# Running the first MLP's first product plainly on the first three token tiles

## The chip, the core and the metric

The kernel runs on one core of one Trainium2 chip. The metric is the device time of one execution in microseconds (us). The median of three runs of the kernel before is 1400.02 us (1398.33 to 1400.51).

The core has five engines with a queue each, which work in order and wait for each other by semaphores: TensorE (PE in the rows, its weight loads PEld), VectorE (DVE), ScalarE (ACT), GpSimd (POOL) and SyncE (SP), which issues all transfers of this kernel.

## The reference

Attention with a softmax over the features of q and over the positions of k, and then two MLPs on its output, all in float32 (the weights of the MLPs arrive as 64-bit floats):

```python
q_s = softmax(q, axis=-1)            # q, k, v: 8 batches, 8 heads, 576 positions, 64
k_s = softmax(k, axis=2)
x   = q_s @ (k_s^T @ v)              # -> 4608 tokens x 512
h   = x @ w_in                       # 512 x 2048
g   = max(h, 0) + alpha * min(h, 0)
x   = g @ w_out                      # 2048 x 512
h   = x @ w2_in                      # 512 x 1024
out = layernorm(h * softmax(h)) * g_ln @ w2_out
```

## The kernel before

**Tiles and stages.** The 4608 tokens are nine tiles of 512 (`NTL`). The first MLP runs in two phases (`ph`), each over half of the 2048 hidden features, and in a phase each tile `i` is worked in two units `u` of 512 features. For a tile and a unit there are a first product (`g1`, into the PSUM banks `ga` and `gx`), the leaky function (`leaky`), a split of its result into two parts (`split_g`, tiles `gg0` and `gg1`), and a second product (`g2`), which adds into four banks `acc`. `finish` copies `acc` to `p_d` in HBM when a tile's two units are done in phase 0; phase 1 adds to that.

**Products in three passes.** All MLP operands are held as a high part in a shorter float format (`F32R`) and the remainder (`put`: ScalarE writes the high part, VectorE or GpSimd subtracts). Each product is high by high, high by low and low by high: three matmuls.

**The first product by seven block products.** `g1` multiplies 512 x 512 blocks with seven products of half-size blocks rather than eight, with block sums of the weights (`S1` to `S4`, made by `w_in_ops`) and of the tokens (`T1` to `T4`, made by `x_prep`). It is issued in four parts, 84 matmuls of 256 columns in all for a tile and unit. `keep` copies three partial results out of PSUM, and VectorE adds them (L248, L256, L258).

**Weights.** `load_w64` brings a 512 KB piece of a 64-bit weight into a raw tile with one transfer on SP's queue, ScalarE turns its high words into floats (L109), and three VectorE instructions (L110 to L112) repair sign and low bits. Then `put` splits it. For phase 0 there are 16 such pieces, four of w_in and four of w_out for each unit. Unit 0's eight are loaded ahead of the tile loop (`boot_w`), and their splits and block sums are put on GpSimd (`G`). Unit 1's eight are loaded in `hook0` in the first three slots of tile 0 (`second_in`, `second_out`), all through one raw buffer: the tag `rn` of the pool `gp`, which has one buffer. `leaky` takes its tile `rn` from the same tag.

**Attention in the slots.** Each tile has eight slots, and the steps of attention for batches 1 to 7 are dealt out to the slots of phase 0. Batch 0 runs ahead of the loop, and tile 0's slots hold all of batch 1 and the start of batch 2. `q_x` makes x and sends it to `x_d` in HBM; for tile 0 it also keeps it in SBUF (`xraw`). The tile `xf`, from which it is sent, has two buffers, and `k_max` of a later batch uses the same two.

**The order.** The program is written in the order of the functions `phase` and `slot`, and a scheduling layer then interleaves the independent pieces on each engine. The order in which the instructions stand on an engine is fixed when the program is built.

## Time and profile before

| | |
|---|---|
| median of three runs | 1400.02 us |
| the profiled execution | 1404.14 us, span 1402.4 us |
| TensorE busy, over the span | 1314.6 us, 94% |
| VectorE busy | 1025.6 us, 73% |
| ScalarE busy | 781.5 us, 56% |
| GpSimd busy | 62.0 us, 4% |
| mean granted clock of TensorE | 0.966 |

A share of the span is an average over stages: batch 0's attention and the weights (to about 50 us), tile 0 (to 197 us), the tiles of phase 0 with attention beside them (to about 512 us), the rest of phase 0, phase 1, and the second MLP. "Busy" of an engine is the union of its instructions' times, and instructions of one engine overlap a little, so the distance between starts is shorter than the length.

### The profile page before, as it was taken

What the parts mean: (1) busy time and instruction counts of PE and PEld (TensorE: products, weight loads), DVE (VectorE), ACT (ScalarE), POOL (GpSimd) and SP (SyncE); (2) the same over time, 40 slices, a digit from 0 to 9 for tenths busy, and PEclk for the clock granted to TensorE, in tenths of its full rate; (3) what the DMA queues carried; (4) which work ended last, traced back from release to release, by engine and by line L of the source; (5) the groups of instructions that cost most, each with busy time, mean ns of one, the idle gap of its engine ahead of it and who ended that gap; (6) DMA issues with size and microseconds to landing.
All of it is one profiled execution on the core that took longest, in us unless ns stands there. A gap on an engine that the chain in (4) does not pass through costs nothing.

```text
span 1402.4 us, 19636 instructions
## 1 busy us (share of the span) xinstructions
PE 1314.6 (94%) x7428; PEld 1131.9 (81%) x7428; DVE 1025.6 (73%) x1730; ACT 781.5 (56%) x1323; POOL 62.0 (4%) x74
## 2 busy tenths in 40 slices
PE   3656899999999999999999999999999999999998
PEld 3544788889898888888888888898788888888886
DVE  6988688889888677797778755545877676766653
ACT  5534655665665656585556645444556455555543
POOL 0612100000000000000000000000000000000000
PEclk8675799999999999999999999999999999999999
DMA  8464224544352433424545422138121111112011
GB/s 181 126 169 144 81 78 127 144 142 119 119 145 65 138 106 128 138 81 141 183 157 195 166 63 88 46 122 274 67 64 38 53 51 41 58 34 61 31 31 30
DMA packets 127919, 148.10 MB, mean 106 GB/s; under 512 B 55504, under 2 KB 94416, under 8 KB 125648
## 3 DMA queue, kind: packets, MB, share of 16 engines
q1 hardware_dynamic: 127824, 146.85, 34.8%
q8 instruction: 58, 0.95, 0.3%
q14 instruction: 37, 0.30, 0.1%
HBM read 99.63 MB, written 47.19 MB: 105 GB/s over the span
## 4 chain that ended last, share of the span: by engine, by line
PE 72%; DVE 10%; DMA 7%; ACT 5%; issue 2%; POOL 1%; SPq 0%; ACTq 0%; DVEq 0%
PE acc L291 7%; PE acc L292 7%; PE acc L290 7%; PE o L897 5%; PE o L899 5%; PE o L898 5%; PE ga L225 4%; PE ga L227 3%; PE ga L226 3%; PE gx L225 2%; PE gx L226 2%; PE gx L227 2%; PE h2a L833 2%; PE h2a L835 2%; PE h2a L834 2%; PE tp L889 2%
## 5 line engine op out<-in xcount | busy, mean ns | idle before, releaser
L291 PE MATMUL acc<-gg,w 128*128 128x512 f32 x576 | 230.2, 400 | 1.9 <-DVE gg L117 1.9
L290 PE MATMUL acc<-gg,w 128*128 128x512 f32 x576 | 229.2, 401 | 2.7 <-ACT gg L116 2.6
L292 PE MATMUL acc<-gg,w 128*128 128x512 f32 x576 | 229.5, 398 | 0.0
L271 DVE SCALAR_TENSOR_TENSOR t<-rn,nalpha,t 128x512 f32<-128x512 f32 x144 | 102.1, 747 | 48.1 <-ACT t L268 47.8
L291 PEld LDWEIGHTS acc<-gg,w 128*128 128x128 f32 x576 | 109.4, 190 | 24.4 <-DVE gg L117 2.7
L292 PEld LDWEIGHTS acc<-gg,w 128*128 128x128 f32 x576 | 109.3, 190 | 24.4
L290 PEld LDWEIGHTS acc<-gg,w 128*128 128x128 f32 x576 | 108.7, 189 | 24.0 <-ACT gg L116 3.2
L267 ACT ACTIVATE rn<-t 128x1024 f32<-128x1024 f32 x72 | 75.7, 1051 | 73.2 <-DVE t L258 72.7
L897 PE MATMUL o<-wo,lt 128*128 128x512 f32 x288 | 114.4, 397 | 0.3 <-ACT lt L116 0.3
L899 PE MATMUL o<-wo,lt 128*128 128x512 f32 x288 | 114.2, 397 | 0.0
L898 PE MATMUL o<-wo,lt 128*128 128x512 f32 x288 | 114.1, 396 | 0.0
L116 ACT ACTIVATE gg<-t 128x1024 fp32r<-128x1024 f32 x72 | 76.4, 1061 | 36.7 <-DVE t L271 35.9
L117 DVE TENSOR_TENSOR gg<-t,gg 128x1024 fp32r<-128x1024 f32 x72 | 87.9, 1220 | 11.3 <-ACT gg L116 11.0
L225 PE MATMUL ga<-xT,w_S 128*128 128x256 f32 x288 | 84.9, 295 | 5.3 <-ACT r L231 4.5
L226 PE MATMUL ga<-xT,w_S 128*128 128x256 f32 x288 | 83.4, 290 | 3.4 <-DVE xT L117 3.4
L117 DVE TENSOR_TENSOR lt<-tp,lt 128x512 fp32r<-128x512 f32 x72 | 46.3, 684 | 51.4 <-ACT lt L116 51.4
L227 PE MATMUL ga<-xT,w_S 128*128 128x256 f32 x288 | 83.3, 289 | 0.5 <-POOL w_S L117 0.3
L268 ACT ACTIVATE t<-t 128x1024 f32<-128x1024 f32 x72 | 75.8, 1052 | 0.7
L876 POOL TENSOR_TENSOR st<-st,mhalf 128x1 f32<-128x1 f32 x36 | 20.6, 573 | 1195.2 <-DVE st L873 876.1
L256 DVE TENSOR_TENSOR t<-ga,r 128x512 f32<-128x512 f32 x36 | 24.8, 688 | 56.5 <-PE ga L227 56.0
L897 PEld LDWEIGHTS o<-wo,lt 128*128 128x128 f32 x288 | 54.2, 188 | 13.6 <-ACT lt L116 0.5
L899 PEld LDWEIGHTS o<-wo,lt 128*128 128x128 f32 x288 | 54.3, 189 | 13.3
(240 smaller groups left out, 3548.7 us busy)
## 6 DMA issues: line engine op xcount, KB each, us to landing
xraw<-x_d SPq DMA_DIRECT2D x17, 1024.0 KB, 4.9
q<-in_q_dram SPq DMA_DIRECT2D x16, 576.0 KB, 5.1
p_d<-pt SPq DMA_DIRECT2D x36, 256.0 KB, 3.2
part<-p_d SPq DMA_DIRECT2D x36, 256.0 KB, 4.1
y_d<-part SPq DMA_DIRECT2D x36, 256.0 KB, 2.5
yraw<-y_d SPq DMA_DIRECT2D x18, 512.0 KB, 3.8
kt<-in_k_dram SPq DMA_DIRECT2D x16, 512.0 KB, 4.2
vt<-in_v_dram SPq DMA_DIRECT2D x64, 128.0 KB, 3.0
```

Of the source, the lines that this page charges most:

```text
L116: S.activation(hi, src, AF.Copy)
L117: eng.tensor_tensor(lo, src, f32(hi), ALU.subtract)
L225: T.matmul(bank[:, z, :], wh, x[:, 0, c, :], start=first and z == 0, stop=False, **go_on)
L226: T.matmul(bank[:, z, :], wh, x[:, 1, c, :], start=False, stop=False, **go_on)
L227: T.matmul(bank[:, z, :], wl, x[:, 0, c, :], start=False, stop=c == 1, **go_on)
L271: V.scalar_tensor_tensor(t[:, j, :], rn[:, j, :], nalpha[:, fg + j:fg + j + 1], t[:, j, :], ALU.mult, ALU.add)
L290: T.matmul(a, wh, g[:, 0, :], start=u == 0 and f == 0, stop=False)
L291: T.matmul(a, wh, g[:, 1, :], start=False, stop=False)
L292: T.matmul(a, wl, g[:, 0, :], start=False, stop=u == NU - 1 and f == FU - 1)
L897: T.matmul(o, lt[:, 0, f, :], wo[f][:, 0, :], start=f == 0, stop=False)
L898: T.matmul(o, lt[:, 0, f, :], wo[f][:, 1, :], start=False, stop=False)
L899: T.matmul(o, lt[:, 1, f, :], wo[f][:, 0, :], start=False, stop=f == KF - 1)
```

## The change

- The first three tiles of phase 0 (`TS = 3`) run `g1` plainly (`g1_plain`): one part for each 128 features, from a chunk of w_in of 512 x 128, with 96 matmuls of 256 columns for a tile and unit in place of 84. ScalarE reads the leaky function's two halves straight from PSUM; `keep` and VectorE's three additions fall away there. `x_prep` makes four operands for these tiles and no sums.
- w_in is loaded by chunks of all 512 rows and 128 columns (`src_chunk`), whose contiguous pieces are 1 KB instead of 2 KB. Three chunks of unit 0 come ahead of the loop; the other 13 pieces of phase 0's weights come in the eight slots of tile 0. Their raw tiles alternate between the tags `T1` and `T2` of the pool `xp`; `rn` is the leaky function's alone.
- All splits of weights run on VectorE. The block sums are made from the chunks in tiles 1 to 3 (`sum_steps`, `s4_step`).
- `q_x` always goes through `xf`, and writes tile 0's operands from PSUM with `put`; `x_prep(0, 0)` is gone.
- Phase 1's 16 weight pieces are loaded one in each slot from tile 6, slot 4, those of w_in first; before, they came two in each slot of tile 7. Unit 0's sums for phase 1 are made in slots 2 to 6 of tile 8, before in 4 to 6.

```diff
+    TS = 3
...
+    def src_chunk(u, f):
+        f0 = (u * FU + f) * P
+        return w1i[:, 2 * f0:2 * f0 + 2 * P].rearrange("(c p) f -> p c f", p=P)
...
+    def load_chunk(u, f, out):
+        w = wsl[0, u, f] if out else wc[u, f]
+        if not staged:
+            w32 = xp.tile([P, 2, N], I32, tag="T4", name="w32a")
+            staged.extend([w32[:, 0, :], w32[:, 1, :], xp.tile([P, N], I32, tag="xt", name="w32b")])
+        raw = xp.tile([P, N, 2], I32, tag=("T1", "T2")[len(staged) % 2], name=f"r{u}_{f}_{int(out)}")
+        src = src_out(0, u, f) if out else src_chunk(u, f)
+        src = load_w64("", src, raw, staged[len(staged) % 3], None if out else KC)
+        staged.append(raw)
+        put(w[:, 0, :], w[:, 1, :], src)
...
+    def whole(dst, u, o):
+        f, c0 = {"A11": (0, 0), "A12": (0, 2), "A21": (2, 0), "A22": (2, 2)}[o]
+        d = dst.rearrange("p (c z f) -> p c z f", c=2, z=2)
+        for z in range(2):
+            w = f32(chunk(u, f + z))
+            V.tensor_tensor(d[:, :, z, :], w[:, 0, c0:c0 + 2, :], w[:, 1, c0:c0 + 2, :], ALU.add)
+    def sum_steps(u):
+        tmp = {}
+        def to(o, src):
+            t = wc[u, o]
+            put(t[:, 0, :], t[:, 1, :], src)
+        def one():
+            tmp["a"] = xp.tile([P, 2, N], F32, tag="T1", name=f"sa_{u}")
+            tmp["s"] = xp.tile([P, 2, N], F32, tag="T2", name=f"ss_{u}")
+            a, s = tmp["a"], tmp["s"]
+            whole(a[:, 0, :], u, "A21")
+            whole(a[:, 1, :], u, "A22")
+            V.tensor_tensor(s[:, 0, :], a[:, 0, :], a[:, 1, :], ALU.add)
+            to("S1", s[:, 0, :])
+        def two():
+            a, s = tmp["a"], tmp["s"]
+            whole(s[:, 1, :], u, "A11")
+            V.tensor_tensor(s[:, 0, :], s[:, 0, :], s[:, 1, :], ALU.subtract)
+            to("S2", s[:, 0, :])
+        def three():
+            a, s = tmp["a"], tmp["s"]
+            V.tensor_tensor(a[:, 0, :], s[:, 1, :], a[:, 0, :], ALU.subtract)
+            to("S3", a[:, 0, :])
+        return [one, two, three]
+    def s4_step(u):
+        a = xp.tile([P, N], F32, tag="xt", name=f"s4a_{u}")
+        s = pp.tile([P, N], F32, tag="part", name=f"s4s_{u}")
+        t = f32(wc[u, "S2"])
+        whole(a, u, "A12")
+        V.tensor_tensor(s, t[:, 0, :], t[:, 1, :], ALU.add)
+        V.tensor_tensor(a, a, s, ALU.subtract)
+        v = a.rearrange("p (c z f) -> p c z f", c=2, z=2)
+        for z in range(2):
+            w = chunk(u, 2 + z)
+            put(w[:, 0, 0:2, :], w[:, 1, 0:2, :], v[:, :, z, :])
...
+    def plain(ph, i):
+        return ph == 0 and i < TS
...
+        def rest():
+            to("B12", b("B12"))
+            to("B22", b("B22"))
+            del xraw[i]
+        return [first, rest] if plain(ph, i) else [first, t1, t2, t3, t4]
...
+    def g1_plain(ph, i, u, f):
+        n = (ph, i, u)
+        z, j = divmod(f, 2)
+        bank = ps_g.tile([P, 2, W], F32, tag="ga" if j == 0 else "gx", name=f"h{f}_{ph}_{i}_{u}")
+        w = chunk(u, f)
+        for c in range(KC):
+            for h in range(2):
+                x = xs[ph, i, f"B{c // 2 + 1}{h + 1}"]
+                out, go_on = bank[:, h, :], dict(skip_group_check=True)
+                T.matmul(out, w[:, 0, c, :], x[:, 0, c % 2, :], start=c == 0 and h == 0, stop=False, **go_on)
+                T.matmul(out, w[:, 0, c, :], x[:, 1, c % 2, :], start=False, stop=False, **go_on)
+                T.matmul(out, w[:, 1, c, :], x[:, 0, c % 2, :], start=False, stop=c == KC - 1, **go_on)
+        if f == 0:
+            tt[n] = [gp.tile([P, 2, N], F32, tag="t", name=f"t{y}_{ph}_{i}_{u}") for y in range(2)]
+        if j == 0:
+            rns[n, z] = gp.tile([P, 2, N], F32, tag="rn", bufs=1, name=f"rn{z}_{ph}_{i}_{u}")
+        rn, t = rns[n, z][:, j, :], tt[n][z][:, j, :]
+        h = bank.rearrange("p h w -> p (h w)")
+        S.activation(rn, h, AF.Relu, scale=-1.0)
+        S.activation(t, h, AF.Relu)
+        fg = (ph * NU + u) * FU + f
+        V.scalar_tensor_tensor(t, rn, nalpha[:, fg:fg + 1], t, ALU.mult, ALU.add)
...
+            xf = at.tile([P, HALF], F32, tag="xf", bufs=2, name=f"xf_{b}_{u}_{j}")
+            S.activation(xf, t, AF.Copy)
             pos = b * SQ + u * HALF
-            xf = None
             done = 0
             while done < HALF:
                 i, o = divmod(pos + done, N)
                 n = min(N - o, HALF - done)
                 if i == 0:
-                    src = x_raw(0)[:, j, o:o + n]
-                    S.activation(src, t[:, done:done + n], AF.Copy)
-                else:
-                    if xf is None:
-                        xf = at.tile([P, HALF], F32, tag="xf", bufs=2, name=f"xf_{b}_{u}_{j}")
-                        S.activation(xf[:, done:], t[:, done:], AF.Copy)
-                    src = xf[:, done:done + n]
-                nc.sync.dma_start(out=x_d[i][:, j, o:o + n], in_=src)
+                    for h in range(2):
+                        a, e = max(o, h * W), min(o + n, (h + 1) * W)
+                        if a < e:
+                            x = x_op(0, 0, f"B{j // 2 + 1}{h + 1}")[:, :, j % 2, a - h * W:e - h * W]
+                            put(x[:, 0], x[:, 1], t[:, done + a - o:done + e - o])
+                nc.sync.dma_start(out=x_d[i][:, j, o:o + n], in_=xf[:, done:done + n])
...
+    w_places(0)
+    load_chunk(0, 0, False)
...
-    ops = w_in_ops(0, 0, first_in, s0, G, G)
...
+    load_chunk(0, 2, False)
...
-    for st in x_prep(0, 0):
-        st()
-    for f in range(FU):
-        w_out_op(0, 0, f, boot_w(f), G)
...
-    def second_in():
-        t = xp.tile([P, KC, N], F32, tag="xraw", name="w_second")
-        for z, o in enumerate(("A11", "A12", "A21", "A22")):
-            raw = gp.tile([P, N, 2], I32, tag="rn", bufs=1, name=f"s64_{o}")
-            second[o] = load_w64(o, src_in(0, 1, o), raw, t.bitcast(I32)[:, z, :], 2)
-        s = xp.tile([P, N], F32, tag="xt", name="w_second_s")
-        for op in w_in_ops(0, 1, second, s, G, V):
-            op()
-    def second_out(f):
-        raw = gp.tile([P, N, 2], I32, tag="rn", bufs=1, name=f"s64_{f}")
-        w = xp.tile([P, N], I32, tag="xt", name=f"s32_{f}")
-        w_out_op(0, 1, f, load_w64(f"o{f}", src_out(0, 1, f), raw, w), G)
...
+    SUMS_AT = [(1, 3), (1, 4), (1, 5), (1, 7), (2, 0), (2, 1)]
...
     def hook0(i, s):
-        if i == 0 and s == 0:
-            second_in()
-        if i == 0 and s in (1, 2):
-            second_out(2 * s - 2)
-            second_out(2 * s - 1)
-        if i == NTL - 2 and s == 0:
+        n = i * SLOTS + s
+        if n < 4:
+            if s == 0:
+                load_chunk(0, 3, False)
+            load_chunk(1, s, False)
+            load_chunk(0, s, True)
+        elif n < 8:
+            load_chunk(1, s - 4, True)
+        if (i, s) in SUMS_AT:
+            sums.pop(0)()
+        if (i, s) == (TS - 1, 3):
+            s4_step(0)
+        if (i, s) == (TS, 0):
+            s4_step(1)
+        if (i, s) == (NTL - 3, 4):
             ps_at.release()
...
+        z = n - (NTL - 3) * SLOTS - 4
+        if 0 <= z < len(NEXT):
...
+    IN_AT = {2: 2, 3: 1, 4: 2, 5: 1, 6: 1}
```

VectorE's queue where the first split of tile 0 stands (`gg_0_0_0`), before. `rk` waits for the last matmuls of batch 1's second half, and `t_0_0_0` needs `rn`:

```order
L110 TENSOR_SCALAR s_1_737<-s_1_737 128x512
L111 SCALAR_TENSOR_TENSOR s_1_737<-s_1_736,s_1_737 128x512
L112 SCALAR_TENSOR_TENSOR s_1_737<-s_1_736,s_1_737 128x512
L407 TENSOR_SCALAR rk_1_1248<-kv_1_1249 64x2 x2
L408 RECIPROCAL rk_1_1248<-rk_1_1248 128x2
L271 SCALAR_TENSOR_TENSOR t_0_0_0_539<-rn_0_0_0_772,nalpha,t_0_0_0_539 128x512 x2
L117 TENSOR_TENSOR xB_0_1_1135<-xraw_1097,xB_0_1_1135 128x512
L117 TENSOR_TENSOR xB_0_1_1138<-xraw_1097,xB_0_1_1138 128x512
L117 TENSOR_TENSOR gg_0_0_0_777<-t_0_0_0_539,gg_0_0_0_777 128x1024
```

The same place in the change. Here `rk` belongs to batch 1's first half; 77 instructions stand from the second `kk` split of batch 0 (not shown) up to this split, 150 before:

```order
L544 TENSOR_SCALAR rk_0_602<-kv_0_603 64x2 x2
L496 TENSOR_TENSOR mx_1_630<-kt 128x256
L545 RECIPROCAL rk_0_602<-rk_0_602 128x2
L122 TENSOR_TENSOR w_1_c_482<-w32a,w_1_c_482 128x512
L548 TENSOR_TENSOR kvF<-kv_0_603,rk_0_602 64x2x64 x2
L498 TENSOR_TENSOR mx_1_630<-mx_1_630,kt 128x256
L116 SCALAR_TENSOR_TENSOR w32a<-r_1_1_662,w32a 128x512
L122 TENSOR_TENSOR kk_601<-kvF,kk_601 128x256
L498 TENSOR_TENSOR mx_1_630<-mx_1_630,kt 128x256
L117 SCALAR_TENSOR_TENSOR w32a<-r_1_1_662,w32a 128x512
L499 TENSOR_TENSOR mx_1_630<-mx_1_630,kt 64x256
L122 TENSOR_TENSOR gg_0_0_0_699<-t_0_0_0_517,gg_0_0_0_699 128x1024
```

So the first split moved ahead of batch 1's second half, and weight pieces stand among the attention steps in front of it.

SP's queue in tile 0, before, with unit 1's pieces `s_A` and `s_0`:

```order
L329 DMA kt<-in_k_dram 64x4x64
L107 DMA s_A_635<-in_moe_w_in_dram 128x2x512
L483 DMA x_d_67<-xf_0_0_810 128x288
L483 DMA x_d_67<-xf_0_1_817 128x288
L338 DMA vt<-in_v_dram 128x4x64 x4
L341 DMA vt<-in_v_dram 64x4x64
L350 DMA q_0_908<-in_q_dram 96x8x192
L107 DMA s_A_641<-in_moe_w_in_dram 128x2x512
L483 DMA x_d_67<-xf_0_2_892 128x288
L483 DMA x_d_67<-xf_0_3_899 128x288
```

The same queue in the change where tile 0's operands leave; `r_` are raw weight pieces. The pieces stand among the sends of x, and two can be under way:

```order
L487 DMA q_1_575<-in_q_dram 96x8x192
L619 DMA x_d_66<-xf_1_1_437 128x224
L619 DMA x_d_67<-xf_1_1_437 128x64
L112 DMA r_0_1_593<-in_moe_w_out_dram 128x1024
L619 DMA x_d_66<-xf_1_2_461 128x224
L619 DMA x_d_67<-xf_1_2_461 128x64
L619 DMA x_d_66<-xf_1_3_471 128x224
L619 DMA x_d_67<-xf_1_3_471 128x64
L112 DMA r_1_0_654<-in_moe_w_in_dram 128x4x256
L112 DMA r_1_1_662<-in_moe_w_out_dram 128x1024
```

Unit 1's pieces moved from behind the loads of k and v for batch 1 to ahead of them, and unit 0's first piece of w_out (`r_0_1`) stands among batch 0's sends.

TensorE's queue at the first matmul of the second product, before:

```order
L467 MATMUL xp_0_1_1220<-qT_0_1_1128,kk_1068 128x288
L468 MATMUL xp_0_1_1220<-qT_0_1_1128,kk_1068 128x288
L399 MATMUL kv_1_1249<-vt,e_1_1208 128x130 x10
L454 MATMUL qtp_0_2_1273<-ident,qe_0_938 128x96 x3
L290 MATMUL acc_0_0_1006<-gg_0_0_0_777,w_0_0_500 128x512
L290 MATMUL acc_0_1_1007<-gg_0_0_0_777,w_0_0_500 128x512
L290 MATMUL acc_0_2_1008<-gg_0_0_0_777,w_0_0_500 128x512
```

And in the change, where it follows a part of unit 1's first product and batch 1's first `kv` instead of the second:

```order
L353 MATMUL h_0_0_1_888<-xB_0_0_370,w_1_c_481 128x256
L536 MATMUL kv_0_603<-vt,e_0_564 128x130 x10
L354 MATMUL h_0_0_1_888<-xB_0_0_370,w_1_c_481 128x256
L352 MATMUL h_0_0_1_888<-xB_0_0_373,w_1_c_481 128x256
L353 MATMUL h_0_0_1_888<-xB_0_0_373,w_1_c_481 128x256
L354 MATMUL h_0_0_1_888<-xB_0_0_373,w_1_c_481 128x256
L352 MATMUL h_0_0_1_922<-xB_0_0_332,w_1_c_482 128x256
L353 MATMUL h_0_0_1_922<-xB_0_0_332,w_1_c_482 128x256
L427 MATMUL acc_0_0_950<-gg_0_0_0_699,w_0_0_250 128x512
L427 MATMUL acc_0_1_951<-gg_0_0_0_699,w_0_0_250 128x512
L427 MATMUL acc_0_2_952<-gg_0_0_0_699,w_0_0_250 128x512
```

The first matmul of the second product is row 164 of TensorE's queue now; it was row 224.

## Rows read from the trace of the kernel before

**Rows 1.** Busy time by stretch: length, busy us (instructions) per engine, clock, DMA share, GB/s.

```profile
28.00:148.00 120.00, 68.92 (x334) 58.52 (x333) 100.25 (x150) 57.61 (x116) 36.53 (x24) 0.66 0.54 148
148.00:197.00 49.00, 46.32 (x259) 39.95 (x260) 37.28 (x53) 28.72 (x42) 2.59 (x2) 0.91 0.18 52
251.00:304.00 53.00, 53.00 (x353) 47.40 (x352) 47.02 (x75) 32.77 (x51) 0.00 (x0) 1.00 0.52 146
```

**Rows 2.** Timeline of the SP queue: start, time to issue, line, transfer.

```profile
78.08 0.39 SPq L107 DMA_DIRECT2D s_A<-in_moe_w_in_dram  x1
...
85.54 0.37 SPq L107 DMA_DIRECT2D s_A<-in_moe_w_in_dram  x1
...
101.72 0.40 SPq L107 DMA_DIRECT2D s_A<-in_moe_w_in_dram  x1
...
110.72 0.33 SPq L107 DMA_DIRECT2D s<-in_moe_w_out_dram  x1
...
130.13 0.56 SPq L107 DMA_DIRECT2D s<-in_moe_w_out_dram  x1
```

**Rows 3.** Timeline of all engines just ahead of the first second-product matmul: start, length.

```profile
138.69 0.69 DVE L112 SCALAR_TENSOR_TENSOR s<-s,s 128x512 int32<-128x512 int32 x1
...
140.49 4.70 PE L399 MATMUL kv<-vt,e 128*128 128x130 f32 x20 [1.66 <-ACT e L386]
140.85 1.05 ACT L267 ACTIVATE rn<-t 128x1024 f32<-128x1024 f32 x1
...
145.68 1.40 DVE L271 SCALAR_TENSOR_TENSOR t<-rn,nalpha,t 128x512 f32<-128x512 f32 x2
...
147.16 1.06 ACT L116 ACTIVATE gg<-t 128x1024 fp32r<-128x1024 f32 x1 [1.04 <-DVE t L271]
...
148.27 1.22 PE L290 MATMUL acc<-gg,w 128*128 128x512 f32 x2 [2.60 <-ACT gg L116]
```

**Rows 4.** Timeline of POOL and VectorE: a split on POOL, and VectorE instructions beside it and later.

```profile
49.84 1.70 POOL L117 TENSOR_TENSOR w_S<-b_s,w_S 128x512 fp32r<-128x512 f32 x1
...
50.35 1.74 DVE L117 TENSOR_TENSOR xT<-xt,xT 128x512 fp32r<-128x512 f32 x1
...
175.27 0.68 DVE L117 TENSOR_TENSOR xT<-xt,xT 128x512 fp32r<-128x512 f32 x1
175.88 0.68 DVE L117 TENSOR_TENSOR xT<-xraw,xT 128x512 fp32r<-128x512 f32 x1
```

**Rows 5.** Timeline of TensorE in a dense stretch, 256 and 512 columns.

```profile
861.08 0.28 PE L226 MATMUL ga<-xT,w_A 128*128 128x256 f32 x1
861.20 0.28 PE L227 MATMUL ga<-xT,w_A 128*128 128x256 f32 x1
861.32 0.40 PE L290 MATMUL acc<-gg,w 128*128 128x512 f32 x1
861.56 0.39 PE L291 MATMUL acc<-gg,w 128*128 128x512 f32 x1
```

**Rows 6.** Timeline of ScalarE: the copies out of finished tiles 0, 1 and 2.

```profile
197.16 1.07 ACT L307 ACTIVATE pt<-acc 128x512 f32<-128x512 f32 x2
...
250.84 1.58 ACT L307 ACTIVATE pt<-acc 128x512 f32<-128x512 f32 x3
...
304.29 0.61 ACT L307 ACTIVATE pt<-acc 128x512 f32<-128x512 f32 x1
```

**Rows 7.** Timeline: batch 0's last product, then batch 1's first half on VectorE and TensorE.

```profile
46.83 0.29 PE L468 MATMUL xp<-qT,kk 128*128 128x288 f32 x1
...
71.95 1.48 DVE L382 TENSOR_TENSOR e<-kt,mb 128x1280 f32<-128x1280 f32 x1
...
78.96 0.33 DVE L407 TENSOR_SCALAR rk<-kv 64x2 f32<-64x2 f32 x2 [1.55 <-PE kv L399]
```

**Rows 8.** Transfers in 0 to 200 us: count, size, median us from issue to landing.

```profile
kt<-in_k_dram SPq DMA_DIRECT2D x7, 512.0 KB, 4.6
...
s_A<-in_moe_w_in_dram SPq DMA_DIRECT2D x4, 512.0 KB, 4.0
s<-in_moe_w_out_dram SPq DMA_DIRECT2D x4, 512.0 KB, 3.6
```

**Rows 9.** Waits of TensorE in 588 to 612: total us, times, longest.

```profile
PE ga L225 <- ACT r L231: 1.8, 3, 1.4
PE ga L225 <- DVE t L256: 1.5, 1, 1.5
```

**Rows 10.** Timeline of VectorE: the split of tile 2's last block.

```profile
286.66 1.22 DVE L117 TENSOR_TENSOR gg<-t,gg 128x1024 fp32r<-128x1024 f32 x1
```

More of the change, by code (lines that the diff above doesn't have):

```diff
@@ L144, in src_out, with w_places, chunk, stat @@
         return w1o[f0:f0 + P, :]
+    wc = {}
+    def w_places(u):
+        for o in (0, 1, "S1", "S2", "S3", 2, 3):
+            wc[u, o] = w_tile(0, u, o if isinstance(o, str) else f"c{o}")
+        for f in range(FU):
+            w_tile(0, u, f)
+    def chunk(u, f):
+        return wc[u, f].rearrange("p s (c f) -> p s c f", c=KC)
+    def stat(ph, u, o, s, c, z):
+        if ph or o in ("S1", "S2", "S3"):
+            return wsl[ph, u, o][:, s, c * W + z * P:c * W + (z + 1) * P]
+        f, c0 = {"A11": (0, 0), "A12": (0, 2), "S4": (2, 0), "A22": (2, 2)}[o]
+        return chunk(u, f + z)[:, s, c0 + c, :]
@@ L172, in x_raw, with x_op @@
         return xraw[i]
+    def x_op(ph, i, o):
+        if (ph, i, o) not in xs:
+            xs[ph, i, o] = xp.tile([P, 2, 2, W], F32R, tag="T3" if o == "B12" else o, name=f"x{o}_{ph}_{i}")
+        return xs[ph, i, o]
+    def plain(ph, i):
+        return ph == 0 and i < TS
     def x_prep(ph, i):
@@ L184, in to @@
         def to(o, src):
[L185 removed]
+            t = x_op(ph, i, o)
             put(t[:, 0], t[:, 1], src)
[L187 removed]
         def first():
@@ L218, in product @@
         ph, i = key
-        w, x = wsl[ph, u, a], xs[ph, i, b]
+        x = xs[ph, i, b]
         for z in range(2):
             for c in range(2):
-                wh, wl = (w[:, s, c * W + z * P:c * W + (z + 1) * P] for s in range(2))
+                wh, wl = (stat(ph, u, a, s, c, z) for s in range(2))
                 first = start and c == 0
@@ L232, in keep @@
         return r
+    rns = {}
+    def g1_plain(ph, i, u, f):
[20 more added lines that the diff above has]
+        V.scalar_tensor_tensor(t, rn, nalpha[:, fg:fg + 1], t, ALU.mult, ALU.add)
     def g1(ph, i, u, part):
         n = (ph, i, u)
+        if plain(ph, i):
+            g1_plain(ph, i, u, part)
+            return
         if part == 0:
@@ L263, in leaky @@
     def leaky(ph, i, u, z):
+        if plain(ph, i):
+            return
         t = tt[ph, i, u][z]
@@ L604, in attention_then_two_mlps @@
     q_tr(0, 0, (0, 1))
-    first_in, first_out = {}, {}
-    def boot_w(o):
-        if o in ("A11", "A21", 0, 2):
-            raw = boot.tile([P, N, 2], I32, tag="w64", name=f"b64_{o}")
-        else:
-            raw = gp.tile([P, N, 2], I32, tag="rn", bufs=1, name=f"b64_{o}")
-        w = boot.tile([P, N], I32, tag="w32", bufs=5, name=f"b32_{o}")
-        if isinstance(o, str):
-            return load_w64(o, src_in(0, 0, o), raw, w, 2)
-        return load_w64(f"o{o}", src_out(0, 0, o), raw, w)
-    for o in ("A11", "A12"):
-        first_in[o] = boot_w(o)
+    load_k(1, 0)
+    load_chunk(0, 1, False)
     q_x(0, 0, (0, 1))
@@ L624, in attention_then_two_mlps @@
     S.activation(nalpha, alpha_sb, AF.Copy, scale=-1.0)
-    for o in ("A21", "A22"):
-        first_in[o] = boot_w(o)
-    s0 = f32(boot.tile([P, N], I32, tag="w32", bufs=5, name="b32_s"))
-    ops = w_in_ops(0, 0, first_in, s0, G, G)
-    ops[0]()
-    ops[1]()
+    load_chunk(0, 2, False)
     q_norm(0, 1)
@@ L634, in attention_then_two_mlps @@
     q_tr(0, 1, (0, 1))
-    for op in ops[2:4]:
-        op()
     q_x(0, 1, (0, 1))
@@ L678, in hook0 @@
             ahead.append(tc.alloc_tile_pool(name="ahead", bufs=1, reuse_waits="tile"))
-        if i == NTL - 2:
-            u, z = divmod(s, 4)
-            for o in (("A11", "A12", "A21", "A22")[z], z):
-                raw = ahead[0].tile([P, N, 2], I32, tag="w64", name=f"a64_{u}_{o}")
-                w = ahead[0].tile([P, N], I32, tag="w32", bufs=4 * FU, name=f"a32_{u}_{o}")
-                src = src_in(1, u, o) if o != z else src_out(1, u, o)
-                second[u, o] = load_w64(f"a{u}{o}", src, raw, w, None if o == z else 2)
-        if i == NTL - 1 and s == 4:
+        z = n - (NTL - 3) * SLOTS - 4
+        if 0 <= z < len(NEXT):
+            u, o = NEXT[z]
+            raw = ahead[0].tile([P, N, 2], I32, tag="w64", name=f"a64_{u}_{o}")
+            w = ahead[0].tile([P, N], I32, tag="w32", bufs=4 * FU, name=f"a32_{u}_{o}")
+            out = not isinstance(o, str)
+            src = src_out(1, u, o) if out else src_in(1, u, o)
+            second[u, o] = load_w64(f"a{u}{o}", src, raw, w, None if out else 2)
+        if i == NTL - 1 and s == 2:
             ready["in", 0] = w_in_ops(1, 0, {o: second[0, o] for o in ("A11", "A12", "A21", "A22")}, gp_s(0), V, V)
-        if i == NTL - 1 and s in (4, 5, 6):
-            for op in ready["in", 0][3 * (s - 4):3 * (s - 3)]:
-                op()
+        if i == NTL - 1 and s in IN_AT:
+            for _ in range(IN_AT[s]):
+                ready["in", 0].pop(0)()
+    IN_AT = {2: 2, 3: 1, 4: 2, 5: 1, 6: 1}
     ready = {}
     def gp_s(u):
-        return ahead[0].tile([P, N], F32, tag="w64", name=f"a_s{u}")
+        return ahead[0].tile([P, N], F32, tag="ws", name=f"a_s{u}")
     def hook_w1(i, s):
```

12 lines of the change are left out of this document (5 added, 7 removed).

## The prediction

> **What bounds the kernel now.** I read the busy times by stretch first, then the timelines. From tile 1 on TensorE has work without a gap: 53.00 of 53 us in tile 2's stretch, at the full clock (2.4 GHz) [rows 1]. The tiles finish 53.7 and 53.5 us apart [rows 6]. Nothing on another engine can shorten such a tile, and more matmuls lengthen it.
>
> From 28 us, where batch 0's k-half is done, to 148 it is otherwise: TensorE is busy 68.92 of 120 us, at a mean granted clock of 0.66, so between its two levels and mostly at 1.2 GHz; VectorE is busy 100.25 us [rows 1]. The second product begins only at 148.27 [rows 3]. The reader is to see why. Unit 1's raw weight pieces go out one at a time: four issues from 78.08 to 101.72, 7.9 us apart, then 9.0 and 19.4 [rows 2], because one raw buffer makes each wait until the one before it has been landed and turned. The leaky function's `rn` uses that same buffer. Its first instruction starts at 140.85, right behind the sixth piece's last VectorE instruction at 138.69; then VectorE stands in `rk` behind `kv` (140.49 and 4.70 us), so that its half of the leaky function comes at 145.68, the split's high part at 147.16, the first matmul at 148.27 [rows 3]. Tile 0's first product had been computed long before.
>
> VectorE is also held up by GpSimd: a 128x512 instruction that starts 0.61 us ahead of the next one takes 1.74 us, not 0.68, while GpSimd splits (1.70 us) [rows 4]. I count 16 VectorE instructions so stretched between 28 and 148 (the one in [rows 4] is typical), 15 us in all.
>
> **The sum, against the profile's own 1404.1 us** (4.1 above the median shown). I follow three times: T1, the first second-product matmul; T2, the end of tile 2, 304.3 now [rows 6]; and the boundary of the phases.
>
> *T1, from 148.3 to 74.* The loads no longer use `rn`, so the leaky function needs only the plain product, and that needs chunks and x. Batch 0's last product starts at 46.83 [rows 7]; I take it as unchanged, since `xf` now paces it by its sends where GpSimd's stretching paced it before. After it come the last pieces of x and their matmuls (some 4 us), the two ScalarE reads and the VectorE sums of two blocks (3 us): the split's input is there at 54. But on VectorE the split stands behind batch 1's first half: maxima, exponent, `rk`. From `e` to `rk` that took 7.0 us [rows 7]. With the maxima and two transposes ahead (some 4 us), starting at 51 because `xf` must be free, `rk` is at 63 and the split, after some 4.6 us of instructions behind it, at 68. The other way: by starts 0.61 us apart for a 128x512 instruction [rows 4], and in proportion for other sizes, the 150 VectorE instructions from batch 0's last `kk` to the first split are 85.6 us of work, and the 77 in the change 39.4. The 120 us of before had 85.6 of work and 15 of stretching, 84%; at that share 39.4 takes 47, which gives 75. Bounds: 68 by the chain alone; 83 if the work goes at 85.6/120. I take 74, near the second way, as ScalarE reads its blocks in order with the loads.
>
> *From T1 to T2, from 156.0 to 180.* Here the change pays. Three counts:
> - TensorE: 96 matmuls of 512 columns at 0.235 and 166 of 256 at 0.12 [rows 5] up to tile 0's end, plus a batch and a half of attention. A batch is 53.6 less 96 x 0.235 and 168 x 0.12, so 11 us. That is 59. Then two tiles at 53.6 plus 24 extra matmuls each (2.9 us): 113. Together 172.
> - VectorE, from the first split to tile 2's last: 179 instructions now, 112 us by starts, in the 138.4 us from 148.25 to 286.66 [rows 10], a share of 0.81 while TensorE was the bound. In the change there are 253. More: attention that stood ahead of the first split (+44, +28.5 us), weight pieces (+18, +9.6), their splits off GpSimd (+17, +9.8), block sums from chunks (+24, +10.6). Less: `x_prep` (-12, -7.4) and `g1`'s additions (-17, -10.4). The sum is 153 us. From the last split to T2 there were 17.6 us [rows 6, 10]; with TensorE waiting for it I take 14. At 0.81 this gives 203, at 0.92 it gives 180, without a gap 167.
> - ScalarE reads PSUM four times per block (0.61 each, as a copy of that size takes [rows 6]) in place of two calls of 1.05 [rows 3] and the `keep`s; it is busy 33 of 53 us [rows 1], which hides it.
>
> VectorE is therefore the likely bound of tile 0 and part of tile 1, TensorE of the rest. Between 172 and 203 I take 180: a queue that is always full can beat 0.81, but it meets `kv` and x's round trip. T2 is 254: 50 us saved.
>
> The splits moved off GpSimd deserve a second look, since VectorE gets 24 of its instructions: 24 x 0.61 is 14.6 us against the 15 us of stretching that end [rows 4], so the move itself is a draw. The Trainium skill (Perfetto Trace Analysis, Optimizing Scalar/DVE Operations) says that a saturated VectorE may gain from giving work to GpSimd, and adds that the two share a read port, so that it might not help. Read without its reservation the rule would make the first split some 15 us later than I have it; the stretched row sides with the reservation.
>
> *The boundary, -3.* TensorE waits 3.3 us in 588 to 612 for `ga` [rows 9], while VectorE and ScalarE are making phase 1's sums late. In the change these pieces come over 16 slots instead of eight and the sums two slots earlier. The bounds are 0 and -4.
>
> Tiles 3 and later are TensorE's and don't change. 1404.1 - 50.3 - 3 = 1350.8; less the 4.1 that the profile lies above the median: **1347**.
>
> **The rivals.**
> - *TensorE dense from T1 on* (12 in 100): VectorE's queue runs without gaps. T1 68 and 172 after it: T2 240, 64 saved, 4 at the boundary: 1332. For it speaks the missing stretching; against it, VectorE's 153 us in 158.
> - *VectorE in step with waits* (17): T1 83 and 203: T2 286, only 18 saved: 1379. For it speaks that VectorE idles for `kv` in tile 0 today [rows 3], and that the x of tile 1 still goes out to HBM and back between two steps.
> - *Slower: SP's queue of raw pieces* (5). Twelve pieces after the first four must pass two buffers, with the loads of k, v, q and the sends of x queued behind each. By [rows 2] a buffer turns in 7.9 us, so a piece passes each 4 us and all in 47; they have about 90 us until tile 0's end. Above 7.3 us each they set tile 0's end, and at 11.8 the 53 us are gone; at 13 the time is 1415. Against it: a transfer of k, in 1 KB pieces as the chunks are, lands in 4.6 us, not much more than w_in's 4.0 in 2 KB pieces and w_out's 3.6 [rows 8]. The Trainium skill (Perfetto Trace Analysis, DMA Optimizations) says that small transfers, under 2 KB, carry a marked overhead each, which speaks against the chunks; taken as a doubling of the 4.0 us, it would raise a piece to 6 us and leave the sum alone.
> - *The start was not the buffer* (4): attention's round trips hold the second product at 148 anyway. Then tiles 1 and 2 cost 5.8 more and the boundary gives 3: 1403 in the median, at the edge of what shows.
>
> **Chances and range.** The forecast holds with 62 in 100, its own range 1335 to 1368. 0.2% (2.8 us) is what a measurement of this kernel can tell from no change. Faster 0.92, same 0.03, slower 0.05. The range 1328 to 1380 takes in the first rival and just the second.
>
> **What would show it.** First second-product matmul at 68 to 83 us; `rn` no longer behind a weight piece; no VectorE instruction of 1.7 us at 512 columns; tile 2's end near 254; tiles 0 to 2 with VectorE busy over 90%; from tile 3 on 53 to 55 us a tile as before; under 1 us of waits near the phase boundary. I am wrong if TensorE waits in tiles 1 and 2 for more than some 10 us, or if SP stands before a raw piece while attention waits for k.

## The result, and the profile after

The changed kernel takes **1365.85 us** (median of 4, 1364.39 to 1367.23), the kernel before 1400.26 in the same comparison: a ratio of 0.9756 (95% interval 0.9739 to 0.9773). The forecast was 1347 in a range of 1328 to 1380: the direction and the range hold, the centre was 19 us too low. The profiled execution took 1367.23, its span is 1365.5.

Timeline of the changed kernel, all engines (start, length, engine, line): the first second-product matmul, the first split's low part, tile 2's last split, and the first copies out of tiles 0, 1 and 2. They answer to [rows 3, 6, 10].

```profile
68.89 1.10 PE L427 MATMUL acc<-gg,w 128*128 128x512 f32 x4
...
73.02 1.21 DVE L122 TENSOR_TENSOR gg<-t,gg 128x1024 fp32r<-128x1024 f32 x1
...
154.91 1.97 ACT L444 ACTIVATE pt<-acc 128x512 f32<-128x512 f32 x3
...
212.91 1.30 ACT L444 ACTIVATE pt<-acc 128x512 f32<-128x512 f32 x2
...
245.88 1.23 DVE L122 TENSOR_TENSOR gg<-t,gg 128x1024 fp32r<-128x1024 f32 x1
...
272.44 1.09 ACT L444 ACTIVATE pt<-acc 128x512 f32<-128x512 f32 x2
```

The reader is to subtract the marks of before. T1 went from 148.3 to 68.9, 79.4 us sooner. T1 to T2 grew from 156.0 to 203.5, so 47.5 are given back. From T2 to the end of the span it was 1098.1 and is 1093.1, 5.0 less. Together that is 36.9, the difference of the two spans. What was given back lies in tile 0: from T1 to its end 86 us; tiles 1 and 2 take 58.0 and 59.5.

Busy time by stretch of the changed kernel (length, then busy us and instructions of PE, PEld, DVE, ACT, POOL; clock, DMA share, GB/s): the start, and tiles 0, 1 and 2. It answers to [rows 1].

```profile
28.00:69.00 41.00, 31.62 (x192) 28.20 (x193) 36.20 (x70) 26.83 (x69) 0.00 (x0) 0.72 0.61 166
69.00:155.00 86.00, 68.70 (x418) 57.60 (x417) 79.61 (x136) 44.60 (x82) 0.00 (x0) 0.92 0.54 151
155.00:213.00 58.00, 56.92 (x386) 51.52 (x385) 50.23 (x83) 33.34 (x60) 0.00 (x0) 1.00 0.42 119
213.00:272.00 59.00, 57.80 (x381) 51.18 (x380) 48.49 (x78) 32.08 (x54) 0.00 (x0) 1.00 0.48 136
```

In tile 0 VectorE is busy 79.61 of 86 us and TensorE 68.70. In tiles 1 and 2 it is the other way round: TensorE is dense, and VectorE idles 7.8 and 10.5 us.

Waits of TensorE in tile 0 of the changed kernel (total us, times, longest):

```profile
PE h L352 <- ACT w_c L121: 4.5, 1, 4.5
PE acc L428 <- DVE gg L122: 3.7, 2, 3.2
PE h L354 <- DVE w_c L122: 2.9, 2, 1.8
PE acc L427 <- ACT w L121: 2.4, 2, 1.6
PE h L353 <- DVE xB L122: 1.2, 2, 1.0
PE xp L603 <- ACT xf L607: 1.2, 2, 0.6
```

No wait stands out. Weights, the leaky function's blocks and x are each late by a little, and ScalarE, named in three of the rows, has 41 idle us in the stretch. That is how one full queue looks from outside: whatever goes through it is late. Whether it is VectorE's queue is for the experiments to say. Not all of the 86 us against TensorE's count of 59 is waiting: 17.3 are idle time, and 9.7 are busy time above the count, at a mean granted clock of 0.92, between its two levels, where the count took the upper one throughout.

### The profile page after: what moved, and what is told of

It is laid out like the page before. It is cut to its first block, busy times and chain, and to the rows that moved or that the text cites. A ratio compares the mean times of both kernels' runs of the same rounds, so it can differ in the third digit from the quotient of the medians.

```text
span 1365.5 us, 19775 instructions
## 1 busy us (share of the span) xinstructions
PE 1305.9 (96%) x7500; PEld 1126.5 (82%) x7500; DVE 1010.6 (74%) x1747; ACT 765.9 (56%) x1322; POOL 22.9 (2%) x48
## 4 chain that ended last, share of the span: by engine, by line
PE 77%; DVE 8%; DMA 8%; ACT 4%; issue 2%; SPq 0%; POOL 0%; DVEq 0%; ACTq 0%; POOLq 0%
PE acc L428 7%; PE acc L429 7%; PE acc L427 7%; PE o L1009 5%; PE o L1011 5%; PE o L1010 5%; PE ga L331 4%; PE ga L333 3%; PE ga L332 3%; PE gx L331 3%; PE gx L333 3%; PE gx L332 3%; PE h2a L945 2%; PE h2a L947 2%; PE h2a L946 2%; PE tp L1001 2%
## 5 line engine op out<-in xcount | busy, mean ns | idle before, releaser
L408 DVE SCALAR_TENSOR_TENSOR t<-rn,nalpha,t 128x512 f32<-128x512 f32 x120 | 85.5, 747 | 38.1 <-ACT t L405 38.0
L404 ACT ACTIVATE rn<-t 128x1024 f32<-128x1024 f32 x60 | 63.1, 1051 | 70.0 <-DVE t L393 69.5
L122 DVE TENSOR_TENSOR gg<-t,gg 128x1024 fp32r<-128x1024 f32 x72 | 87.8, 1219 | 12.0 <-ACT gg L121 11.7
L331 PE MATMUL ga<-xT,w_S 128*128 128x256 f32 x240 | 68.8, 287 | 1.7 <-ACT r L337 1.5
L333 PE MATMUL ga<-xT,w_S 128*128 128x256 f32 x240 | 67.7, 282 | 0.0
L332 PE MATMUL ga<-xT,w_S 128*128 128x256 f32 x240 | 67.5, 281 | 0.0
L1009 PEld LDWEIGHTS o<-wo,lt 128*128 128x128 f32 x288 | 54.2, 188 | 13.6 <-ACT lt L121 0.5
L1011 PEld LDWEIGHTS o<-wo,lt 128*128 128x128 f32 x288 | 54.3, 189 | 13.3
L1010 PEld LDWEIGHTS o<-wo,lt 128*128 128x128 f32 x288 | 54.2, 188 | 13.2
L405 ACT ACTIVATE t<-t 128x1024 f32<-128x1024 f32 x60 | 63.2, 1053 | 0.6
L352 PE MATMUL h<-xB,w_c 128*128 128x256 f32 x192 | 57.1, 302 | 6.6 <-ACT w_c L121 4.5
```

The lines of the kernel that those rows point to most:

```text
L122: eng.tensor_tensor(lo, src, f32(hi), ALU.subtract)
L331: T.matmul(bank[:, z, :], wh, x[:, 0, c, :], start=first and z == 0, stop=False, **go_on)
L332: T.matmul(bank[:, z, :], wh, x[:, 1, c, :], start=False, stop=False, **go_on)
L333: T.matmul(bank[:, z, :], wl, x[:, 0, c, :], start=False, stop=c == 1, **go_on)
L408: V.scalar_tensor_tensor(t[:, j, :], rn[:, j, :], nalpha[:, fg + j:fg + j + 1], t[:, j, :], ALU.mult, ALU.add)
L1009: T.matmul(o, lt[:, 0, f, :], wo[f][:, 0, :], start=f == 0, stop=False)
```

## The experiments

Theory: the gain is T1 (the leaky function is freed from the one raw buffer, and the plain product needs no sums), and a part of it is given back in tile 0 because VectorE is full there. Rivals: the gain came from GpSimd, whose splits no longer stretch VectorE's instructions; the loss in tile 0 comes from SP's queue, in which raw pieces stand behind sends of x; the buffer was not what held the start. Each edit makes the scheduling layer order the queues anew, so a run can change more than its edit. Marks of two profiles of the same kernel differ too: in a second one of the changed kernel T1 is 66.5 and the end of tile 0 154.74. "End of tile 0" is the first copy out of it. "Tile 4" below is the first copy out of tile 4, 413.73 us before and 381.03 in the changed kernel: from there on the kernels do the same work but for the boundary of the phases.

**The buffer alone, in the kernel before.**

```diff
-    pp = tc.alloc_tile_pool(name="pp", bufs=KC)
+    pp = tc.alloc_tile_pool(name="pp", bufs=KC // 2)
-            raw = gp.tile([P, N, 2], I32, tag="rn", bufs=1, name=f"s64_{o}")
+            raw = pp.tile([P, N, 2], I32, tag="part", name=f"s64_{o}")
```

(The same for the w_out pieces; a tile of the pool now holds two of the former halves, with the users of the pool written accordingly.) 

> The kernel before with one thing changed: unit 1's eight raw pieces get two buffers of their own in the pool of the part tiles, so that the leaky function's rn shares its buffer with none of them. The split theory (the buffer was one brake, but the first product by seven products, its sums and a whole batch of attention stand ahead of the first split in VectorE's order): 85.6 us of VectorE work and some 15 of stretching still stand between 28 us and the first second-product matmul, so it cannot come before 129; I expect 129 to 138, tile 2's end 285 to 296, the time 1380 to 1392 where before takes 1400. If the buffer alone was what held the start, as the prediction's words have it: first matmul 74 to 100, tile 2's end 240 to 265, time 1345 to 1370. If the buffer was nothing: 146 to 149 and 1400.

Measured: 1382.39 us (1378.99 to 1382.75), ratio 0.9881 (0.9853 to 0.9908). Timeline of this kernel (all engines): the last SP issues of unit 1's pieces, the first second-product matmul, the copy out of tile 2. Behind it the busy time from 28 us to that matmul.

```profile
79.94 0.38 SPq L107 DMA_DIRECT2D s_A<-in_moe_w_in_dram  x1
...
85.50 2.56 SPq L107 DMA_DIRECT2D s<-in_moe_w_out_dram  x2
...
103.91 0.39 PE L290 MATMUL acc<-gg,w 128*128 128x512 f32 x1
...
104.45 4.24 SPq L107 DMA_DIRECT2D s<-in_moe_w_out_dram  x2
...
280.86 2.04 ACT L313 ACTIVATE pt<-acc 128x512 f32<-128x512 f32 x4
```

```profile
28.00:104.00 76.00, 45.07 (x226) 40.13 (x227) 69.96 (x101) 42.27 (x82) 34.64 (x23) 0.61 0.52 149
```

The fourth w_in piece went out at 101.72 [rows 2]; here it is at 79.94, and T1 falls from 148.3 to 103.9. So the buffer did hold the start: 44 of the 79 us. The edit gives the pieces two buffers and frees `rn` in one, and does not part the two. In time it is worth 17.1 us, where the whole change is worth 34.4. My expectation of T1 missed in both forms: I had held that the 150 VectorE instructions of 28 to 148 must all stand ahead of the first split. In 28 to 104 there are 101; the others came in behind. Tile 2's end, 280.86, missed both ranges too. The time fell into its range for a wrong reason: T1 came 25 us before the earliest of the split theory, and T1 to T2 took 177.0 in place of 156.0.

**Splits of phase 0's weights back on GpSimd.** `put(..., src)` became `put(..., src, G)` in `load_chunk`. 

> The changed kernel with the splits of phase 0's 16 weight pieces back on GpSimd, as before. A draw, as the prediction has it: 16 instructions (9.8 us) leave VectorE, and by 15 us per 24 splits the stretching takes 10 us back: 1363 to 1370 where the change takes 1366, tile 0's end within 4 us of 154.9. If the relief of the full VectorE counts (a saturated engine gains from giving work away): tile 0's end 145 to 149, 1356 to 1360. If leaving GpSimd was the real source of the gain: tile 0's end after 165, 1376 or more. In each case VectorE instructions of 1.7 us at 512 columns come back beside the splits.

Measured: 1362.1 us (1357.71 to 1363.59), ratio 0.9729 (0.9701 to 0.9758); tile 0 ends at 147.90, tile 4 at 376.89. Timeline of this kernel, POOL and DVE, at one split:

```profile
77.66 1.28 POOL L122 TENSOR_TENSOR w_c<-w32b,w_c 128x512 fp32r<-128x512 f32 x1 [5.51 <-ACT w_c L121]
77.88 2.15 DVE L122 TENSOR_TENSOR gg<-t,gg 128x1024 fp32r<-128x1024 f32 x1
```

The instruction beside the split takes 2.15 us in place of 1.21. The 1.7 us at 512 columns that I expected did not come back: the longest there is 1.37. And only 8 VectorE instructions are stretched, by 5.5 us in all, while 16 (9.8 us) are taken away: 4.3 of relief, and tile 4 is 4.1 sooner. Tile 0's end is where the relief was expected (though only one of its four copies goes out at 147.90, the others from 150.14), the time between that and the draw. The rival that the gain came from GpSimd is out, since the sign is the other way. In time the intervals of the two kernels overlap, so the relief itself is not shown.

**Raw pieces on GpSimd's queue.** In `load_w64`, phase 0's transfers are issued by `nc.gpsimd` in place of `nc.sync`. 

> The changed kernel with phase 0's 16 raw weight pieces issued from GpSimd's queue, so that none of them stands behind SP's sends of x, which wait for ScalarE's xf. If VectorE's work is what fills tile 0: nothing or a little, tile 0's end at most 4 us sooner (VectorE idles 6.4 us between 69 and 155), 1362 to 1367. If the loss in tile 0 is SP's order: tile 0's end 137 to 147, 1350 to 1358.

Measured: 1368.72 us (1364.21 to 1370.06), ratio 0.9776 (0.9748 to 0.9805). Timeline of the queues, first of the changed kernel, then of this one: the last raw piece.

```profile
136.53 0.55 SPq L112 DMA_DIRECT2D r<-in_moe_w_out_dram  x1
```

```profile
122.15 0.53 POOL L112 DMA_DIRECT2D r<-in_moe_w_out_dram  x1 [5.09 <-issue]
```

The last piece goes out 14 us sooner, and tile 0 ends at 152.93, 2 us sooner; tile 4 is at 381.61, no sooner. The time lies above both expectations, but its interval overlaps that of the changed kernel (0.9739 to 0.9773). T1 is 75.9 here, 7 us later: VectorE has 85 instructions from 28 us to T1 in place of 70, so a part of its work stands ahead of T1 instead of behind it, and tile 0's end hardly moves. SP's order did delay the pieces, but that is not what sets tile 0's end.

**Less work on VectorE.**

```diff
-        V.scalar_tensor_tensor(w, lo, 29, w, ALU.logical_shift_right, ALU.bitwise_or)
+        if name:
+            V.scalar_tensor_tensor(w, lo, 29, w, ALU.logical_shift_right, ALU.bitwise_or)
```

> The changed kernel without the third VectorE instruction in turning a raw weight piece of phase 0 (the one that puts in the lowest 3 of the 23 mantissa bits; the weights of phase 0 lose those bits, nothing else is left out). 16 instructions of 0.61 us leave VectorE, 3 of them before the first split, 13 in tile 0: 9.8 us. If VectorE is the bound of tile 0: first second-product matmul 1 to 2 us sooner, tile 0's end 7 to 10 us sooner (145 to 148), 1356 to 1359. If waits or the queues set tile 0's end: under 3 us, 1363 to 1366.

Measured: 1354.18 us (1353.6 to 1357.64), ratio 0.9683 (0.9657 to 0.9709). The start and tile 0's stretch of this kernel by windows, then the copy out of tile 0 from its ScalarE timeline:

```profile
28.00:71.00 43.00, 32.35 (x213) 29.55 (x212) 37.28 (x71) 29.27 (x73) 0.00 (x0) 0.74 0.66 177
71.00:143.00 72.00, 62.41 (x378) 53.12 (x377) 64.99 (x109) 39.10 (x70) 0.00 (x0) 0.91 0.60 168
```

```profile
143.12 1.31 ACT L445 ACTIVATE pt<-acc 128x512 f32<-128x512 f32 x2 [2.41 <-PE acc L430]
```

Tile 0 ends 11.8 us sooner, tile 4 10.4 (370.59) and the median 11.7: slightly more than the 9.8 us of work that left VectorE. This is the test of the theory, and it holds: in tile 0 a microsecond of VectorE is about a microsecond of the kernel. The excess comes with the new order: from 28 us to tile 0's end VectorE has 180 instructions in place of 206, so ten more than the 16 fell out of that stretch. T1 was expected 1 to 2 us sooner and came 2.1 later (71.0). The edit shortens the turn of each piece as well, not only VectorE's queue. Against that as the reason speak the run above, in which earlier pieces gave next to nothing, and the one with later attention below, which leaves the turn as it is and still ends tile 0 sooner.

The same two rows can be read for every version. From 28 us to tile 0's end VectorE is busy 115.8 of 127 us in the changed kernel and 102.3 of 115 here. In all variants of the changed kernel, those below too, this share is 0.89 to 0.92, with tile 0's end anywhere from 142 to 166; before it was 0.81 (137.5 of 169) [rows 1]. That fits a tile that ends when VectorE has done its part.

**The lowest bits on ScalarE.** For phase 0's pieces alone; those of phase 1 keep the three instructions (the branch is not shown).

```diff
+            S.activation(lo, lo.bitcast(mybir.dt.uint32), AF.Copy, scale=7 * 2.0 ** -32)
-        V.tensor_scalar(w, w, 3, MAGN, ALU.logical_shift_left, ALU.bitwise_and)
-        V.scalar_tensor_tensor(w, hi, SIGN, w, ALU.bitwise_and, ALU.bitwise_or)
-        V.scalar_tensor_tensor(w, lo, 29, w, ALU.logical_shift_right, ALU.bitwise_or)
+            V.scalar_tensor_tensor(w, w, 3, lo, ALU.logical_shift_left, ALU.bitwise_or)
+            V.scalar_tensor_tensor(w, hi, SIGN, w, ALU.bitwise_and, ALU.bitwise_or)
```

> The changed kernel with the third VectorE instruction of a raw weight piece of phase 0 moved to ScalarE (it makes the lowest 3 mantissa bits by a scaled copy, rounded to 0 to 7, and the shift of the high part takes them in; the lowest bit of a weight may differ by a rounding). VectorE loses 16 instructions as in the run without those bits (that took 1354), ScalarE gains 16 of some 0.6 us, while it is busy 44.6 of the 86 us of tile 0 after the first second-product matmul. If VectorE's work alone is the bound: 1353 to 1358, tile 0's end at 143 to 147. If ScalarE's order is close behind, half of that is lost: 1359 to 1363.

Measured: 1362.84 us (1362.37 to 1366.64), ratio 0.9748 (0.9721 to 0.9776); tile 0 ends at 149.64, 5.3 sooner. That is the second range, but not for its reason. What was exchanged: of the changed kernel the VectorE instruction that went (the group on one of its tiles, then one in the timeline with the instruction behind it), of this kernel the ScalarE group that came.

```profile
L115 DVE TENSOR_SCALAR w32a<-w32a 128x512 int32<-128x512 int32 x10 | 4.1, 416 | 0.0
```

```profile
128.25 0.42 DVE L115 TENSOR_SCALAR w32a<-w32a 128x512 int32<-128x512 int32 x1
128.59 1.48 DVE L519 TENSOR_TENSOR e<-kt,mb 128x1280 f32<-128x1280 f32 x1
```

```profile
L116 ACT ACTIVATE r<-r 128x512 int32<-128x512 uint32 x15 | 10.1, 672 | 0.0
```

What VectorE lost is the shift, 0.42 us long and 0.34 by starts, not one of the two of 0.68 (0.61 by starts): 16 x 0.34 is 5.4 us, and tile 0's end shows 5.3. I had priced it as the one that was left out in the run above. ScalarE's 10 us cost nothing up to there. But tile 4 is only 2.6 us sooner (378.42) and the median 3.0, with overlapping intervals: tile 1 took 60.8 us, not 58.0, and no run says why.

**Attention one slot later.** `hs = SLOTS * (b - 1) + s - 6` became `... + s - 5`. 

> The changed kernel with attention of batch 2 and the later ones one slot later (of eight in a tile). One step of a batch's ten leaves tile 0. If VectorE's work sets tile 0's end: tile 0 ends 1 to 4 us sooner, and the time is 1362 to 1365, less what tile 1 gives back. If the waits behind attention's round trips set it, the same steps come later and the x of the next tile with them: 1366 to 1372.

Measured: 1361.29 us (1357.09 to 1363.12), ratio 0.9726 (0.97 to 0.9751); tile 0 ends at 147.14, 7.8 sooner, tile 4 at 370.43, more than expected. The profiled execution is the fastest of the four (1357.09); in the medians the gain is 4.6 us, and the intervals just overlap. So work that merely leaves tile 0 for a tile in which VectorE has room looks like a gain; the step takes some of TensorE's work with it too (65.4 busy us in tile 0, not 68.7), which this run does not part.

**Two plain tiles.** `TS = 2`, and the six sum steps in slots 0 to 5 of tile 1. 

> The changed kernel with two plain tiles in place of three: the block sums are made in slots 0 to 5 of tile 1, six slots sooner at the end, and tile 2 runs the first product by seven products. By the count of matmuls tile 2 is 2.9 us shorter (24 matmuls of 0.12). If VectorE still has room in tile 1 (it was busy 58.2 of 60 us in 140 to 200): 1362 to 1364. If VectorE is full there too, the 24 instructions of the sums (10.6 us) that fall into tile 1 lengthen it by 3 to 8 us: 1366 to 1372, tile 1's end after 215, with TensorE waiting for x or gg in tile 1.

Measured: 1365.3 us (1362.82 to 1367.21), ratio 0.9758 (0.9735 to 0.978). The copies come in other groups here (tile 0 at 166.26, tile 1 at 208.45), so tile 4 is the mark: 376.29, 4.7 sooner in the profile, which is not in the median. Inconclusive: between the two expectations.

**The old order at the boundary.** Phase 1's pieces again two in a slot in tile 7, its sums in slots 4 to 6 of tile 8. 

> The changed kernel with the old order at the boundary of the phases (phase 1's raw pieces two to a slot in the last tile but one, the first sums at slots 4 to 6 of the last tile). If the boundary is worth what the prediction gave it: 1367 to 1370, 2 to 5 us more than the change, all of it between 560 and 620 us in waits of TensorE for ga, and nothing before 510 us. If that schedule was worth nothing: within 1 us of the change, 1365 to 1367.

Measured: 1366.79 us (1364.56 to 1369.78), ratio 0.9771 (0.9746 to 0.9795). Waits of TensorE in 560 to 615, of the changed kernel, then of this one:

```profile
PE ga L331 <- DVE t L391: 3.8, 1, 3.8
```

```profile
PE ga L331 <- ACT r L337: 1.8, 3, 1.4
PE ga L331 <- DVE t L391: 1.5, 1, 1.5
PE ga L333 <- DVE w_S L122: 0.2, 1, 0.2
PE gx L333 <- DVE w_S L122: 0.2, 1, 0.2
```

3.8 us in the one and 3.7 in the other, with other names. So the new order took nothing off TensorE's waits there. In time the two differ by 0.9 us in the medians and by 2.1 in the ratios, inside the noise: a gain from the new order is not shown.

**Together, on one chip.** The changed kernel again, and three combinations of the edits above: attention later with the splits on GpSimd, with the bits on ScalarE, and with both.

> The changed kernel itself, for a comparison in one place with the three versions below: 1364 to 1368.

> Attention one slot later, and the 16 splits on GpSimd: each took VectorE's work out of tile 0. By itself the one gave 4.6 us, the other 3.8 (9.8 us of splits less 5.5 us of stretching). If both come off the same full queue and TensorE is not yet dense in tile 0: they add, 1355 to 1359. If one slot later has already left TensorE waiting for ScalarE and x alone: 1359 to 1363.

> Attention one slot later, and the lowest mantissa bits made on ScalarE (16 VectorE instructions of 0.42 us go, by themselves 3.0 us in the median): if they add, 1356 to 1360; if ScalarE's queue sets tile 0's end instead, 1361 to 1365.

> All three reliefs of VectorE together: by their sum 11.4 us below the changed kernel, 1352 to 1357, while VectorE stays the bound. TensorE's own work from the first second-product matmul to tile 0's end was some 66 us in these runs, so no version can end tile 0 before 134; if TensorE becomes the bound of tile 0 the gain stops at about 1355.

| | median us | ratio to before (95%) | end of tile 0, tile 4 |
|---|---|---|---|
| the changed kernel | 1365.71 | 0.9769 (0.9747 to 0.979) | 154.74, 380.26 |
| later, GpSimd | 1358.83 | 0.9718 (0.9694 to 0.9742) | 148.42, 373.23 |
| later, ScalarE | 1354.68 | 0.9684 (0.9664 to 0.9704) | 142.19, 364.78 |
| all three | 1355.15 | 0.9688 (0.9671 to 0.9705) | 142.21, 365.52 |

Busy time by stretch in the second combination, tile 0 and tile 1:

```profile
67.00:142.00 75.00, 63.23 (x397) 54.81 (x398) 68.14 (x118) 45.96 (x83) 0.00 (x0) 0.93 0.61 169
142.00:200.00 58.00, 57.81 (x392) 52.06 (x391) 55.52 (x92) 33.62 (x60) 0.00 (x0) 1.00 0.44 119
```

Later attention and the bits on ScalarE do at least add: 11.0 us below the changed kernel, where alone they gave 4.6 and 3.0, and their interval lies below its own. That is a little below the range for adding (1356 to 1360). Tile 0 takes 75 us in place of 86, and VectorE (68.14) and TensorE (63.23) now stand close. GpSimd adds nothing on top (1355.15 against 1354.68; inside the range for all three). With later attention alone it comes to 1358.83, at the upper end of the range for adding. The second combination leaves no part out, though the lowest bit of a weight of phase 0 may differ by a rounding, and it beats both kernels: 44.6 us below before.

## Why the prediction came out as it did

*T1, 74 (68 to 83): the number is right, 68.9, in part by luck.* That the one raw buffer held the start is shown by the run of the buffer alone for 44 of the 79 us. The other 35 come with the rest of the change; no run parts the plain product from the loads by chunks. But what ends the wait now is not what the working followed. These are lines of the changed kernel: batch 0's last product, the first split's high part, and TensorE's next use of that split.

```profile
52.97 0.30 PE L605 MATMUL xp<-qT,kk 128*128 128x288 f32 x1
...
58.81 1.06 ACT L121 ACTIVATE gg<-t 128x1024 fp32r<-128x1024 f32 x1 [0.28 <-DVE t L364]
...
74.29 0.50 PE L428 MATMUL acc<-gg,w 128*128 128x512 f32 x1 [0.45 <-DVE gg L122]
```

Batch 0's last product was taken as unchanged at 46.83 and comes 6 us later. The high part, which the first four matmuls need, is there at 59.9, and VectorE's split only at 73.02, near the 75 of the second way. The first matmul comes between, at 68.9, because of its place in TensorE's own queue: from 57 to 68.9 TensorE is busy 11.85 of 11.90 us with first products and steps of attention that stand ahead of it. The working had TensorE waiting for VectorE there.

*T1 to T2, 180: the term that was mis-sized.* It measured 203.5, the upper of its own bounds, and with the smaller errors it makes the 19 us: 5.1 less at T1, 23.5 more here, 2.0 less after T2, and 2.7 from the distance of the profile to the median. The mechanism was named rightly ("VectorE is therefore the likely bound of tile 0 and part of tile 1"), but the value was picked at a share of 0.92 without a reason from a row. The marks show by how much: from T1 to the first split's low part 4.1 us, which the sum had at nothing; 172.9 from there to tile 2's last split where 153/0.92 is 166; and 26.6 from there to T2, not 14. The count of VectorE's work was good: 255 instructions and 154.7 busy us stand in the 172.9, where the sum had 253 and 153. By tiles it is clearer. TensorE's count for tile 0 was 59, and it took 86, with VectorE busy 93% of it: 27 of the 31.5 us above TensorE's count are there. Tiles 1 and 2 were counted at 113 and took 117.5, 5.8 of it the 48 plain matmuls extra. There TensorE is dense: it waits 2.3 us in all from 155 to 272, and never for a split. Why the time from the last split to T2 grew from 17.6 to 26.6 is not shown; the split was not late before either, with TensorE busy 53.00 of 53 us in tile 2 [rows 1]. The sum had treated three tiles as one stretch with one share for VectorE, and they are one tile bound by VectorE and two by TensorE.

*The splits, a draw: nearly.* No VectorE instruction of the changed kernel is stretched. With the splits on GpSimd 5.5 us of stretching stand against 9.8 of relief, since 8 of 16 splits met an instruction that they slowed, not two in three as before. In the medians it is some 4 us with overlapping intervals, and nothing on top of the second combination. The Trainium skill (Perfetto Trace Analysis, Optimizing Scalar/DVE Operations) holds that work may be moved off a saturated VectorE to ScalarE, or to GpSimd with a doubtful result; the runs agree with both halves of that.

*The boundary, -3: not shown.* Putting the old order back changes neither TensorE's waits there nor, clear of noise, the time. The 5 us that the profile shows after T2 are mostly elsewhere, 3.4 of them behind phase 1's first `part` addition (645.41 before, 611.94 now); the old order at the boundary keeps most of that (T2 to the end 1094.6). A second profile of the changed kernel had 1091.0 in place of 1093.1, so single profiles differ by 2 us here. The cause stays open.

*The 4.1 us of the profile above the median* were 1.4 in the changed kernel: that is the 2.7 above.

*The rivals.* TensorE dense from T1 on: no, 15.9 us of waits in the rows of tile 0 above. VectorE in step with waits: its 203 came true, with a T1 of 69 in place of 83. SP's queue: its own limit was passed, as the pieces stood some 9.4 us apart (eight gaps from 61.39 to 136.53) and it had said that 7.3 decides. Yet on another queue the last piece went out 14 us sooner, and tile 0 ended only 2 us sooner. A limit on a spacing does not say what the spacing costs. The pieces themselves were not slow: 4.3 us in 1 KB pieces, 4.0 before in 2 KB [rows 8]. The start was not the buffer: no.

*The signs.* As said: no weight piece before `rn`, no VectorE instruction of 1.7 us at 512 columns, 54.5 and 54.1 us for tiles 3 and 4. Not as said: T2 at 272 and not near 254; VectorE over 90% in tile 0 alone (93%, then 87% and 82%); 3.8 us of waits at the boundary, not under 1. Neither sign of being wrong came: TensorE waits 2.3 us in tiles 1 and 2, and no wait of VectorE for k shows from 28 to 155 us. None of the signs looked at tile 0, where the time went.
